# Probabilities times values by pairs of heads, 64 stationary columns each, in a fused attention and ELU feed-forward kernel

## The chip, the core and the metric

The kernel runs on one core of a Trainium2 chip. The core has five engines with queues of their own, each worked off in order: TensorE (PE, with its loads of stationary operands shown as PEld), VectorE (DVE), ScalarE (ACT), GpSimd (POOL) and SyncE (SP), which in this kernel issues all DMAs. The metric is the device time of one execution in microseconds, the median of several runs.

## The reference

Causal attention with a decay bias that is summed along the sequence, then a feed-forward layer with ELU on its result:

```python
B, H, S, D = q.shape                     # 8, 8, 576, 64
scores = q @ k.T / sqrt(D)
cum = cumsum(maximum(s, 0), -1)          # s: one number per head and position
bias = -(cum[..., :, None] - cum[..., None, :])
scores = where(causal, -1e9, scores + minimum(bias, 0))
attn = exp(scores - max(scores)); attn /= sum(attn) + 1e-9
x = (attn @ v) laid out as (4608 tokens, 512)
h = x @ w_in                             # 512 -> 2048
g = where(h > 0, h, exp(minimum(h, 0)) - 1)
out = g @ w_out                          # 2048 -> 512
```

All inputs and the output are float32.

## The kernel before

**How the order is made.** Every piece of work is written as an operation with a priority, one or more ways to do it (an engine, a planned cost in ns, and the code), the buffers it reads and those it writes (`op`). `Plan.issue` then runs a list scheduler on the host while the program is built: it picks, again and again, the operation that could start first by its planned times, takes the cheapest way, and writes the instructions down in this order. The chip sees only the result: a fixed order on each engine. A DMA is planned with a cost on SP (`SP_COST`, 430 ns, or 1250 ns for a transposing one) and a landing time (`LAG`, 1800 ns, plus bytes over `RATE`); a later operation that needs the data is placed after that. If the chip lands the data later than planned, the engine that reads it stands, and so does all that stands behind it in that engine's queue.

**Attention.** The first 320 positions of the first three batches (`Low`) are done in float32. All else goes by units (`Unit`): for each batch and pair of heads one unit for the first 64 positions of both heads (`h` is None), then one for each head with its blocks of 128 query rows: four blocks in batches 3 to 7 ("full", 20 pairs), the last two in batches 0 to 2 ("late", 12 pairs). A unit is prepared (loads of k and q, split into high and low parts), scored (`scoring`: matmuls into a PSUM bank, mask and minimum on DVE at L967, exponential on ACT at L972, then in `halved` the probabilities as two float16 halves, high on POOL, DVE or ACT, low mostly on DVE at L1025, interleaved into a tile `p16`, and turned by a transposing DMA into a tile `T`, L383), and weighed (`weighing`): the product with the values. There are two `T` buffers (`N_T`).

**The product.** `pair_values` splits the values of a pair of heads into float16 high and low parts, `v[:, head, key block, part, 64]`. In `weighing`, `keys(kb)` takes both parts of one head, 128 columns, as the stationary operand, and moves the high and then the low half of the probabilities past it. So PSUM rows 0 to 63 of `av` collect what the high values give and rows 64 to 127 what the low values give, and each head has 9 matmuls (L1084): two for each of four blocks of 128 keys, and one for the last 64 keys, whose halves lie in one tile. `halves` then adds the two halves of `av` into the half of the result tile `x` that belongs to the head: one instruction that scales and moves the other half (ACT at L1143 or DVE at L1145), one on DVE that scales and adds its own (L1148). After the second head `x` goes to DRAM.

**Scales.** `group_values` loads the values of a whole batch (a group) into a buffer of their own, `va`, kept in the place of a weight tile that is no longer needed: four such places (`w_all`) in turn. `scales_of` finds the group's largest value for a power of two: a maximum for each partition on DVE (`own`, L593), out to DRAM (`aside`), back into all partitions (`every`), and there the maximum and its exponent on DVE (L596, L598, L582).

**Feed-forward.** Tokens go in 12 chunks of 384. The weights are split into float16 parts, and each product is three matmuls: `hidden` (L1304, 384 columns), the ELU on ACT (L1268, L1275), `h` and `gg` on DVE and ACT (L1313, L1317, L1322), `project` (L1341, 512 columns), and the copy-out (L1372, L1373). The first chunk is done in float32 (L1288, L1333). These matmuls have the lowest priority: they fill PE where attention isn't ready.

## Time and profile before

| | |
|---|---|
| median of 3 runs | 1136.91 us (1136.84 to 1140.44) |
| profiled execution | 1139.71 us, its span 1137.9 us |
| mean granted TensorE clock | 0.981 |
| busy time of PE, DVE, ACT, POOL | 1052.2, 897.2, 651.3, 509.0 us |
| AV matmuls (L1084, tile `T`) | 576, 20 x 2 x 9 in full units, 12 x 2 x 9 in late ones |
| feed-forward matmuls in float16 | 2112 of 384 columns, 1584 of 512 |

The full units run from about 135 to 807 us, the late ones to 1023 us, and what is left of the feed-forward to the end. A row of a table of groups gives the line, the engine, the operation, what is written and read with its shape, the count, then busy time in us and mean ns of one; a matmul's mean is longer than its pace, because matmuls overlap. A row of waits names who waited for whom, with the total in us, how often, and the longest. An engine's name with a q behind it (SPq) is its sequencer.

### The profile page before, as it was taken

The page shows a single profiled execution, that of the slowest core. Times are in us where ns is not written, and L with a number is a line of the kernel's source. Part 1 is how long each engine was busy: PE and PEld are TensorE (multiplying, and loading weights), DVE is VectorE, ACT ScalarE, POOL GpSimd, SP SyncE. Part 2 cuts the span into 40 slices and gives each one's busy share as a digit, 9 for nine tenths or more (in the row PEclk, how much of TensorE's full clock was granted, in tenths as well). Part 3 has the DMA queues.
Part 4 walks back from the last instruction along what each step waited for, and adds up shares of the span by engine and source line. Part 5 has one row for each costly group of instructions (what it writes and reads, how often), then busy time and mean ns, then how long its engine had stood idle before and what let it go on. Part 6 is the DMA issues. An engine that isn't in the chain of part 4 may idle for free. (4 is left out here: it accounts for less than half of the span.)

```text
span 1137.9 us, 19124 instructions
## 1 busy us (share of the span) xinstructions
PE 1052.2 (92%) x5650; PEld 618.8 (54%) x5650; DVE 897.2 (79%) x2250; ACT 651.3 (57%) x1513; POOL 509.0 (45%) x756
## 2 busy tenths in 40 slices
PE   8799998798799989999899879999999999999998
PEld 7676554354455545545455535555556555555554
DVE  7788987898877878988698778888899898962433
ACT  4686765555454656556466555666665565554443
POOL 5542345925445454645455435555564553520000
PEclk9899999999999999999999989999999999999999
DMA  7687886473675685665666556566657666540000
GB/s 168 184 233 214 210 225 149 126 195 96 150 144 87 171 168 137 135 165 126 125 160 157 115 150 147 132 142 150 140 137 164 129 156 148 115 110 10 29 1 28
DMA packets 307160, 157.22 MB, mean 138 GB/s; under 512 B 226648, under 2 KB 281840, under 8 KB 307056
## 3 DMA queue, kind: packets, MB, share of 16 engines
q1 hardware_dynamic: 307056, 156.00, 58.3%
q8 instruction: 45, 0.74, 0.3%
q14 instruction: 59, 0.48, 0.2%
HBM read 80.38 MB, written 19.32 MB: 88 GB/s over the span
## 5 line engine op out<-in xcount | busy, mean ns | idle before, releaser
L1304 PE MATMUL h<-xh,wp 128*128 128x384 f16 x1408 | 394.1, 328 | 25.1 <-DVE gg L1322 24.9
L1341 PE MATMUL o<-wp,gg 128*128 128x512 f16 x1584 | 394.9, 386 | 2.3 <-DVE gg L1319 1.8
L1304 PEld LDWEIGHTS <-wp 128*128 128x128 f16 x2112 | 195.9, 98 | 176.5 <-issue 41.0
L1341 PEld LDWEIGHTS <-gg 128*128 128x128 f16 x1584 | 148.1, 99 | 160.7 <-issue 11.7
L1304 PE MATMUL h<-xl,wp 128*128 128x384 f16 x704 | 230.5, 327 | 3.8 <-POOL xl L1254 3.7
L972 ACT ACTIVATE p<-p,mn 128x192 f32<-128x192 f32 (+1 forms) x232 | 144.3, 622 | 89.7 <-DVE mn L967 86.1
L1268 ACT ACTIVATE g<-h,cs 128x384 f32<-128x384 f32 x176 | 101.9, 579 | 142.1 <-PE h L1304 140.0
L1313 DVE SCALAR_TENSOR_TENSOR h<-g,cs,h 128x384 f32<-128x384 f32 x176 | 108.5, 617 | 77.9 <-ACT g L1275 76.6
L1025 DVE SCALAR_TENSOR_TENSOR p<-p,sm,p 128x512 f16<-128x512 f32 (+3 forms) x224 | 164.6, 754 | 4.1 <-POOL p L1017 2.5
L1317 ACT ACTIVATE gg<-h 128x384 f16<-128x384 f32 x160 | 78.2, 488 | 102.5 <-DVE h L1313 101.1
L1017 POOL TENSOR_SCALAR p<-p,sm 128x64 f16<-128x64 f32 (+3 forms) x130 | 88.0, 683 | 94.9 <-DVE sm L978 57.4
L964 PE MATMUL sc<-kh,qs 128*128 128x192 f32 (+2 forms) x272 | 117.0, 433 | 10.6 <-DVE mn L967 6.5
L967 DVE CUSTOM_DVE_ANT_0 p<-sc,maskw 128x192 f32<-128x192 f32 (+1 forms) x232 | 108.9, 480 | 16.2 <-PE sc L964 13.7
L1322 DVE SCALAR_TENSOR_TENSOR gg<-h,gg 128x384 f16<-128x384 f32 x176 | 97.0, 551 | 19.3 <-ACT gg L1317 17.2
L964 PE MATMUL sc<-k,q 128*128 128x192 f32 (+2 forms) x272 | 84.1, 314 | 11.8 <-DMA q<-qs 11.8
L1084 PE MATMUL av<-T,v 128*128 128x256 f16 (+5 forms) x576 | 84.0, 292 | 2.2 <-DMA T<-p 2.2
L1084 PEld LDWEIGHTS <-v 128*128 128x128 f16 x576 | 55.7, 99 | 40.1 <-issue 7.8
L1275 ACT ACTIVATE g<-g 128x384 f32<-128x384 f32 x143 | 74.7, 522 | 4.1
L411 POOL TENSOR_TENSOR k<-stk,kh 64x576 fp32r<-64x576 f32 x46 | 69.8, 1517 | 10.4 <-ACT kh L392 8.2
L964 PEld LDWEIGHTS sc<-kh,qs 128*128 128x128 f32 x272 | 52.1, 192 | 40.9 <-DVE mn L967 15.8
L390 POOL TENSOR_SCALAR qs<-stq 128x512 fp32r<-128x512 f32 (+1 forms) x39 | 23.3, 597 | 90.0 <-PE sc L964 45.3
L402 POOL TENSOR_SCALAR v<-va,scales 128x320 f16<-128x320 f32 x43 | 24.8, 583 | 84.7 <-PE av L1084 76.6
(174 smaller groups left out, 1571.8 us busy)
## 6 DMA issues: line engine op xcount, KB each, us to landing
stk<-in_kT_dram SPq DMA_DIRECT2D x64, 288.0 KB
va<-in_vb_dram SPq DMA_DIRECT2D x32, 320.0 KB
stq<-in_qT_dram SPq DMA_DIRECT2D x40, 256.0 KB
w_i<-in_w_in_dram SPq DMA_DIRECT2D x16, 512.0 KB
w_o<-in_w_out_dram SPq DMA_DIRECT2D x16, 512.0 KB
out_dram<-ost SPq DMA_DIRECT2D x32, 256.0 KB
x_dram<-x_None SPq DMA_DIRECT2D x20, 288.0 KB
q<-qs SPq DMA_DIRECT2D x40, 128.0 KB
```

The costliest lines, as they stand in the source:

```text
L964: pe_.matmul(view(sc.v[:, :cw]), l, r, start=n == 0, stop=n == len(pairs) - 1)
L967: op(prio, [("DVE", 84 + dve_p(cw), lambda i=i, sc=sc: dve.tensor_tensor_reduce(pt.v[:, i * cw : (i + 1) * cw], sc.v[:, :cw], mv(i * cw, c ...
L972: op(prio, [("ACT", 480 + w / 1.2, lambda: act.activation(pt.v[:, :w], pt.v[:, :w], AF.Exp, bias=mn.v[:, n - 1 : n], scale=-1.0, accum_out ...
L1017: ("Pool", 160 + 1.04 * n, lambda part=part: pool.tensor_scalar(part(t16, 0), own(part), sm.v[:, r], 1.0, ALU.mult, ALU.mult)),
L1025: ("DVE-SB", dve_2(n), lambda part=part: dve.scalar_tensor_tensor(part(t16, 1), own(part), sm.v[:, r], part(t16, 0), ALU.mult, ALU.subtract)),
L1084: op(prio, [("PE", cost, lambda m=m, operands=operands: pe_.matmul(av.v[:, dst], *operands(), start=first and m == 0, stop=last and m == l ...
L1268: op(side, [("ACT", act_c(TC) + (0 if native else 90), lambda: act.activation(g.v[:, :TC], hp.v[:, :TC], AF.Exp, scale=1.0 if native else ...
L1304: pe_.matmul(hp.v[:, :TC], weight_part(f, 0, part)[1]()[:, c * P : (c + 1) * P], xx.v[:, c, :TC], start=(c == 0 and m == 0), stop=(c == NC ...
L1313: op(side, [("DVE", dve_p(TC), lambda: dve.scalar_tensor_tensor(hp.v[:, :TC], g.v[:, :TC], by(2 if sign[0] else 1), hp.v[:, :TC], ALU.mult ...
L1317: ("ACT", act_c(TC), lambda: act.activation(gg.v[:, 0, :TC], hp.v[:, :TC], AF.Copy, scale=2.0**-DOWN)),
L1322: op(side, [("DVE", dve_p(TC), lambda: dve.scalar_tensor_tensor(gg.v[:, 1, :TC], hp.v[:, :TC], 2.0**-DOWN, gg.v[:, 0, :TC], ALU.mult, ALU. ...
L1341: pe_.matmul(acc[i].v, gg.v[:, g, tb], weight_part(f, 1, part)[1](), start=(f == 0 and m == 0), stop=(f == NF - 1 and m == 2),)
```

## The change

Five things are changed, in one edit.

1. The product of probabilities and values is made once for a pair of heads. The stationary operand is now one part of one head's values, 64 columns; head 0 writes PSUM rows 0 to 63 and head 1 rows 64 to 127 of one bank, so that each half lies on the 64 columns of the array that belong to these rows. The matmuls of the two heads alternate. For each block of 128 keys there are three products a head (high values with high probabilities, high with low, low with high; low with low is left out), for the last 64 keys two. All 28 matmuls are one operation of the planner.
2. `av` then holds the finished result of both heads, in the rows where `x` wants them: one scaled copy of 128 rows (ACT or DVE, L1136 to L1140) in place of two instructions for each head. `halves` stays for the first 64 positions, without a scale.
3. `T` may also lie in the places of the third and fourth weight tile, once these were in use as weights; the values of groups then use only the first two (`% 2` in `group_values`).
4. The two DMAs of `scales_of` are planned with landing times of 5000 and 4500 ns instead of 1800, so is the write of the decay sums (5000).
5. Some planned costs and the planner's rule for VectorE's and GpSimd's shared use of a port (`PORT_LEAD`, 300 before, now 240 and 120) have other numbers.

```diff
-    PORT, PORT_LEAD = ("DVE-SB", "Pool"), 300.0
+    PORT_LEAD = {"DVE-SB": 240.0, "Pool": 120.0}
...
-        load(15, lambda: aux_dram.v[:, 0], sp, [(aux, 0)], [(aux_dram, 0)], NB * S * 4)
+        load(15, lambda: aux_dram.v[:, 0], sp, [(aux, 0)], [(aux_dram, 0)], NB * S * 4, lag=5000.0)
...
-        op(prio, [("DVE-SB", 30.0 + 70 * n, largest)], used, [own])
-        load(prio, lambda: aside.v.rearrange("n p -> p n"), lambda: own.v, [own], [aside], P * n * 4)
+        op(prio, [("DVE-SB", 60.0 + 70 * n, largest)], used, [own])
+        load(prio, lambda: aside.v.rearrange("n p -> p n"), lambda: own.v, [own], [aside], P * n * 4, lag=5000.0)
         load(prio, lambda: every.v, lambda: aside.v.rearrange("n p -> (n p)").partition_broadcast(P),
-             [aside], [every], P * P * n * 4)
-        op(prio, [("DVE-SB", 300.0 + 130 * n, exponents)], [every], [own, (scales, dst)])
+             [aside], [every], P * P * n * 4, lag=4500.0)
+        op(prio, [("DVE-SB", 500.0 + 130 * n, exponents)], [every], [own, (scales, dst)])
...
-        home = w_parts[NG - 1] if at == 0 else w_all[(at - 1) % NG]
+        home = w_parts[NG - 1] if at == 0 else w_all[(at - 1) % 2]
...
-        u.pt = plan.buf(sb, [P, 1 + (u.turns[u.last] - 1) * u.n_blocks, P], F16, f"T_{u.tag}", tag="T", bufs=N_T)
+        u.pt = plan.buf(sb, [P, 1 + (u.turns[u.last] - 1) * u.n_blocks, P], F16, f"T_{u.tag}", tag="T", bufs=N_T,
+                        others=[(w_all[g].key[1], 1, lambda n: n > 0) for g in range(2, NG)], always=True)
...
-            def own():
-                return u.values.v[:, u.h, kb].rearrange("p a d -> p (a d)")
-            used = [(u.pt, i) for i in range(i0, last)] + [(u.values, (m, u.h)) for m in range(2)]
-            pairs = [(used, lambda m=m: (own(), part(m))) for m in range(1 + (kb < last))]
-            products(pe16(c), pairs, dst, kb == 0, kb == last)
-            if kb == last:
-                halves(prio, u.back, u.h, wq, u.x_part((u.h, first)), HB + P * first, av, 0)
...
+        if u.h == 0:
+            return []
+        pair = (u.first_head, u)
...
+                for kb in range(last + 1):
+                    dst = slice(wq - columns(kb), wq)
+                    for m, v in ((0, 0), (1, 0), (0, 1)) if kb < last else ((0, 0), (0, 1)):
+                        for w in pair:
+                            pe_.matmul(
+                                av.v[w.h * HB : (w.h + 1) * HB, dst], w.values.v[:, w.h, kb, v], part(w, kb, m),
+                                start=kb == 0 and m == 0 and v == 0, stop=kb == last and v == 1,
+                            )
+            cost = sum((3 if kb < last else 2) * (pe16(columns(kb)) + 4) for kb in range(last + 1))
+            op(prio, [("PE", 200 + cost, step)],
+               [(w.pt, i) for w in pair for i in u.blocks] + [(u.values, (m, h)) for m in range(2) for h in range(2)],
+               [av])
...
+                ("ACT", act_c(wq) + 90, lambda: act.activation(
+                    x.v[:, cols], av.v[:, :wq], AF.Copy, scale=scales.v[:, back])),
+                ("DVE", dve_p(wq), lambda: dve.tensor_scalar(
+                    x.v[:, cols], av.v[:, :wq], scales.v[:, back], None, ALU.mult)),
```

Three places show the new order. The names: `av_5_1_0` is the product of batch 5, pair 1, head 0; `T_5_1_0` its turned probabilities; `h_3_13` and `wp_3` belong to the feed-forward; the last number of a name only tells tiles apart. On PE, where the product of batch 5, pair 1 begins, before:

```order
L1304 LDWEIGHTS wp_3_2378
L1304 MATMUL h_3_13_5233<-xh_2276,wp_3_2378 128x384
L1084 LDWEIGHTS v_5_1_0_0_4731
L1084 MATMUL av_5_1_0_0_5248<-T_5_1_0_0_5117,v_5_1_0_0_4731 128x512
L1084 LDWEIGHTS v_5_1_0_0_4731
L1084 MATMUL av_5_1_0_0_5248<-T_5_1_0_0_5117,v_5_1_0_0_4731 128x512
L1084 LDWEIGHTS v_5_1_0_0_4731
L1084 MATMUL av_5_1_0_0_5248<-T_5_1_0_0_5117,v_5_1_0_0_4731 128x448
```

and after:

```order
L1312 LDWEIGHTS wp_2_2275
L1312 MATMUL h_3_11_5245<-xh_2252,wp_2_2275 128x384
L1126 LDWEIGHTS v_5_1_0_0_4532
L1126 MATMUL av_5_1_1_0_5264<-T_5_1_0_0_5003,v_5_1_0_0_4532 64x512
L1126 LDWEIGHTS v_5_1_0_0_4532
L1126 MATMUL av_5_1_1_0_5264<-T_5_1_1_0_5146,v_5_1_0_0_4532 64x512
L1126 LDWEIGHTS v_5_1_0_0_4532
L1126 MATMUL av_5_1_1_0_5264<-T_5_1_0_0_5003,v_5_1_0_0_4532 64x512
L1126 LDWEIGHTS v_5_1_0_0_4532
L1126 MATMUL av_5_1_1_0_5264<-T_5_1_1_0_5146,v_5_1_0_0_4532 64x512
```

The two heads' T now alternate row by row, into 64 rows each of one bank; before, head 1's nine came some 120 rows later, after other work, with a bank of their own. (In the changed kernel the feed-forward's lines stand 8 lower: L1312 is what L1304 was.)

On SP, around the scales of the last group (`own_18`), before:

```order
L378 DMA stq_7_0_None_0_7302<-in_qT_dram 128x128
L378 DMA aside_18_7314<-own_18_7306 128x1
L378 DMA stv_7_0_None_0_7329<-in_vb_dram 128x64
L378 DMA every_18_7348<-aside_18_7314 128x128
L378 DMA k2_0_192<-aux_dram_219 1x576 x2
L378 DMA q2s_184<-qs_7_0_None_0_7379 64x128
```

and after:

```order
L378 DMA aside_18_9709<-own_18_9703 128x1
L378 DMA q2_0_190<-qs_1_0_0_2_9711 64x256
L378 DMA stk_1_0_1_2_9728<-in_kT_dram 128x576
L378 DMA stq_1_0_1_2_9735<-in_qT_dram 128x2x128
L383 DMA_TRANSPOSE T_0_3_0_2_9788<-p16_0_3_0_2_2_9774 128x8x128
L378 DMA every_18_9802<-aside_18_9709 128x128
```

Four DMAs now stand between the way out and the way back, where one stood; and with two buffers for groups in place of four the trip is made in batch 0's late units, not in batch 6. On DVE, 17 rows stood between L593 and L596 of this group and now 28 do.

On DVE, where the result of batch 5, pair 1 is copied out, before:

```order
L1313 SCALAR_TENSOR_TENSOR h_3_15_5375<-g_3_15_5413,cs_3_3336,h_3_15_5375 128x384
L1145 TENSOR_SCALAR x_5_1_None_0_5143<-av_5_1_1_0_5416,scales_71 64x512
L1148 SCALAR_TENSOR_TENSOR x_5_1_None_0_5143<-av_5_1_1_0_5416,scales_71,x_5_1_None_0_5143 64x512
L1322 SCALAR_TENSOR_TENSOR gg_3_15_5440<-h_3_15_5375,gg_3_15_5440 128x384
L977 TENSOR_SCALAR sm_5_2_0_0_5356<-sm_5_2_0_0_5356 128x4
```

and after:

```order
L978 RECIPROCAL sm_5_2_0_0_5194<-sm_5_2_0_0_5194 128x4
L1019 TENSOR_SCALAR p16_5_2_0_0_0_5301<-p0_82,sm_5_2_0_0_5194 128x2x128
L1140 TENSOR_SCALAR x_5_1_None_0_4957<-av_5_1_1_0_5264,scales_71 128x512
L1025 SCALAR_TENSOR_TENSOR p16_5_2_0_0_0_5301<-p0_82,sm_5_2_0_0_5194,p16_5_2_0_0_0_5301 128x2x128
L1025 SCALAR_TENSOR_TENSOR p16_5_2_0_0_1_5303<-p1_84,sm_5_2_0_0_5194,p16_5_2_0_0_1_5303 128x3x128
```

The two instructions for head 1 (and two more for head 0, earlier) became one. Of these 32 copies the planner puts 20 on ACT and 12 on DVE, and it moves some work from POOL to DVE: over the program POOL has 112 instructions fewer, DVE 32 fewer and ACT 11 more.

More of the change, by code (lines that the diff above doesn't have):

```diff
@@ L208, in issue @@
                     if b.others and (b.always or not busy):
-                        for key, bufs, *most in b.others:
-                            if most and taken[key] > most[0]:
+                        for key, bufs, *rule in b.others:
+                            if rule and not rule[0](taken[key]):
                                 continue
@@ L237, in issue @@
             end = start + cost
-            if engine in self.PORT:
+            if engine in self.PORT_LEAD:
                 port = end
@@ L1130, in weighing, with part, heads, step @@
-        return [lambda kb=kb: keys(kb) for kb in range(last + 1)]
-    def halves(prio, back, h, n, dst, c0, av, a0):
+            return P * (last - i0) - HB * half
+        def part(w, kb, m):
+            c = columns(kb)
+            if kb == last:
+                return w.pt.v[:, 0, P - c :]
+            end = (1 + (2 * kb + m + 1) * w.n_blocks) * P
+            return w.pt.v.rearrange("p u q -> p (u q)")[:, end - c : end]
+        def heads():
+            def step():
+                for kb in range(last + 1):
[10 more added lines that the diff above has]
+               [av])
+            x, label = u.x_part(("rows", first))
+            back, cols = slice(u.back, u.back + 1), slice(HB + P * first, HB + P * first + wq)
+            op(prio, [
+                ("ACT", act_c(wq) + 90, lambda: act.activation(
+                    x.v[:, cols], av.v[:, :wq], AF.Copy, scale=scales.v[:, back])),
+                ("DVE", dve_p(wq), lambda: dve.tensor_scalar(
+                    x.v[:, cols], av.v[:, :wq], scales.v[:, back], None, ALU.mult)),
+            ], [av, (scales, u.back)], [(x, label)])
+            load(prio, lambda: x_dram.v[u.b, u.j][:, u.cols], lambda: x.v[:, u.cols], [x],
+                 [(x_dram, u.piece)], P * (u.cols.stop - u.cols.start) * 4)
@@ L1134, in halves @@
+        return [heads]
+    def halves(prio, h, n, dst, c0, av, a0):
         x = dst[0]
@@ L1136, in halves @@
         cols, here = slice(c0, c0 + n), slice(a0, a0 + n)
[L1137 to L1150 removed]
+        psum_copy(prio, n, lambda: x.v[own, cols], lambda: av.v[other, here], [av], [dst])
+        op(prio, [("DVE", dve_p(n), lambda: dve.tensor_tensor(
+            x.v[own, cols], av.v[own, here], x.v[own, cols], ALU.add))], [av], [dst])
     def attention():
```

37 lines of the change are left out of this document (9 added, 28 removed).

## The prediction, made before the changed kernel ran

> **What bounds the kernel now.** I read the busy shares first, then a table of two stretches, the waits, the timeline around the longest waits, and the chain of work for rates. The shares of the span and two of the rows in 40 slices:
>
> ```profile
> span 1137.9 us, 19124 instructions
> PE 1052.2 (92%) x5650; PEld 618.8 (54%) x5650; DVE 897.2 (79%) x2250; ACT 651.3 (57%) x1513; POOL 509.0 (45%) x756
> PE   8799998798799989999899879999999999999998
> DVE  7788987898877878988698778888899898962433
> ```
>
> PE is the bound: 1052 us busy of 1138. So there are two ways to gain: less PE work, or less of its 86 us of idle time. The stretch with full and late units, and the rest after the last of them (columns: width, then busy time and count of PE, PEld, DVE, ACT, POOL; the clock; the DMA share; GB/s):
>
> ```profile
> 165.00:1024.00 859.00, 795.05 (x4346) 454.39 (x4345) 725.88 (x1792) 493.75 (x1108) 434.77 (x594) 0.98 0.62 142
> 1024.00:1138.00 114.00, 109.85 (x591) 57.54 (x588) 38.27 (x65) 47.56 (x89) 2.15 (x3) 1.00 0.05 17
> ```
>
> 64 us of the idle time lie in the first, where DVE is busy for 84% too; the second is almost pure PE. What is waited for (total us, times, longest):
>
> ```profile
> PE h L1304 <- DVE gg L1322: 24.9, 12, 7.0
> PE sc L964 <- DMA q<-qs: 11.8, 3, 4.2
> PE sc L964 <- DVE mn L967: 6.5, 9, 1.6
> PE sc L964 <- DVE pc_None L1035: 3.3, 1, 3.3
> PE av L1084 <- DMA T<-p: 2.2, 3, 0.8
> DVE own L596 <- DMA every<-aside: 18.0, 5, 6.4
> SPq L378 <- DMA aside<-own: 33.1, 7, 6.8
> ```
>
> PE waits mostly for DVE, and DVE itself stands for 18 us behind the exponents of a group's scales. The timeline shows how that reaches PE (start, duration; in brackets the idle time before and who ended it), once at 644 and once at 275 us:
>
> ```profile
> 643.90 0.37 SPq L378 DMA_DIRECT2D aside<-own  x1
> 644.32 0.43 SPq L378 DMA_DIRECT2D stv_None<-in_vb_dram  x1
> 650.92 0.33 SPq L378 DMA_DIRECT2D every<-aside  x1
> ...
> 649.90 0.18 DVE L978 RECIPROCAL sm<-sm 128x4 f32<-128x4 f32 x1
> 656.51 0.29 DVE L596 TENSOR_REDUCE own<-every 128x1 f32<-128x128 f32 x1 [6.43 <-DMA every<-aside]
> ...
> 659.92 0.48 PE L1304 MATMUL h<-xh,wp 128*128 128x384 f16 x1 [6.97 <-DVE gg L1322]
> ...
> 274.69 0.44 SPq L378 DMA_DIRECT2D aside<-own  x1
> 282.49 0.33 SPq L378 DMA_DIRECT2D every<-aside  x1
> 287.60 0.29 DVE L596 TENSOR_REDUCE own<-every 128x1 f32<-128x128 f32 x1 [2.91 <-DMA every<-aside]
> 289.82 0.74 PE L964 MATMUL sc<-kh,qs 128*128 128x448 f32 x1 [3.35 <-DVE pc_None L1035]
> ```
>
> The way out to DRAM takes 7.0 and 7.8 us from issue until SP may issue the way back, which takes another 5.6 and 5.1 us. The planner allows 2 x (0.43 + 1.8) = 4.5 us for the 12.6 to 12.9 us. Since queues run in order, SP stands from 644.75 to 650.92 with every later load behind it, DVE stands 6.43 us with h and gg behind it, and PE loses 6.97 us.
>
> **The AV products.** The chain of work gives their pace, the other rows the tail of a short matmul and the loads of stationary columns (busy us, mean ns):
>
> ```profile
> 733.16 1.28 PE av L1084 x9
> 860.12 0.85 PE av L1084 x9
> ...
> L1084 PE MATMUL av<-T,v 128*128 128x64 f16 x64 | 12.3, 193 | 0.0
> ...
> L1084 PEld LDWEIGHTS <-v 128*128 128x128 f16 x576 | 55.7, 99 | 40.1 <-issue 7.8 <-DMA T<-p 1.7 <-DMA k2s<-aux_dram 1.1
> L1288 PEld LDWEIGHTS h<-x,wa 128*128 128x128 f32 x128 | 23.7, 194 | 13.3 <-issue 4.4
> ...
> 9.19 5.43 PEld L1404 LDWEIGHTS scratch<-ident 128*128 128x128 f32 x48
> ```
>
> A head of four blocks moves 2 x (512 + 448 + 320 + 192) + 64 = 3008 columns in 1.28 us, one of two blocks 2 x (3 x 256 + 192) + 64 = 1984 in 0.85 us: 0.43 ns a column, weight loads hidden. A pair costs 2.56 us (20 pairs) or 1.70 us (12 pairs), 71.6 us in all. After, a pair of heads needs 28 half-width matmuls instead of 18 full ones, because high and low values are no longer in one stationary tile (low times low is dropped): 6 x 1472 + 4 x 64 = 9088 columns, or 6 x 960 + 4 x 64 = 6016.
>
> No row of this trace has a stationary tile of 64 columns, so I bound it. If the two halves of the array work side by side, half the columns count: 1.95 and 1.29 us, that is -0.61 x 20 - 0.41 x 12 = -17.1 us. If they don't, 3.91 and 2.59 us: +1.35 x 20 + 0.89 x 12 = +37.7 us. I take side by side, since the two heads of each round write disjoint output rows from disjoint columns of the array and nothing in the rows makes one wait for the other, but with two costs of its own. First, two weight loads a round: the f32 row has 48 loads of 128 columns in 5.43 us, 0.11 us each, so 64 columns are at most 0.055 and a round at least 0.11 us. That leaves the wide rounds alone (0.22, 0.19, 0.14 us) and stretches those of 192 and 64 columns: 3 x (0.22 + 0.19 + 0.14) + 3 x 0.11 + 2 x 0.11 = 2.20 us, and for two blocks 9 x 0.11 + 3 x 0.11 + 2 x 0.11 = 1.54 us; -0.36 x 20 - 0.16 x 12 = -9.1 us. If half-width f16 loads are as quick as the f16 row (99 ns in all against 194), they hide and -17.1 stands; I take the f32 price because the loads then decide and the careful end costs only 8 us. Second, entering and leaving half-width work may empty the array: a 64-column matmul lasts 193 ns and streams for 28, so a break costs up to 0.165 us; one for each of 32 blocks is 5.3 us. The term is -9.1 + 5.3 = -3.8 us, between -17.1 and +37.7.
>
> The Trainium skill bears on both costs. Its page "TensorEngine Tiling (Array Packing)", section "Restrictions", says that column tiling disables Fast Weight Load, which speaks against this change: by it the f32 price holds and the term is -3.8; were it wrong, about -11.8. The f16 and f32 rows above agree that there are two speeds; no run so far shows which one a half tile gets. The same page, section "Key Properties", says that a change of tiling mode drains the array, which is the break; no row here shows one. The page "TensorE: Matmul & The Clock Gate", Part 3, gives a span of one matmul plus about 4 ns for each further tile; by that alone the term is -17.1 and the sum near 1108 us, which stands among the rivals.
>
> **Copying the result out.** What two instructions for each head did becomes one for a pair:
>
> ```profile
> L1148 DVE SCALAR_TENSOR_TENSOR x_None<-av,scales,x_None 64x512 f32<-64x512 f32 x40 | 29.9, 747 | 4.3 <-ACT x_None L1143 3.5
> L1148 DVE SCALAR_TENSOR_TENSOR x<-av,scales,x 64x256 f32<-64x256 f32 x24 | 11.6, 481 | 1.4 <-ACT x L1143 0.9
> L1145 DVE TENSOR_SCALAR x_None<-av,scales 64x512 f32<-64x512 f32 x14 | 10.5, 747 | 8.5 <-PE av L1084 8.3
> L1145 DVE TENSOR_SCALAR x<-av,scales 64x256 f32<-64x256 f32 x7 | 3.3, 477 | 1.3 <-PE av L1084 1.2
> L1143 ACT ACTIVATE x_None<-av,scales 64x512 f32<-64x512 f32 x26 | 17.8, 684 | 11.6 <-PE av L1084 11.3
> L1143 ACT ACTIVATE x<-av,scales 64x256 f32<-64x256 f32 x17 | 8.0, 470 | 9.8 <-PE av L1084 9.6
> ...
> L1025 DVE SCALAR_TENSOR_TENSOR p<-p,sm,p 128x64 f16<-128x64 f32 x30 | 12.0, 400 | 0.8 <-POOL p L1017 0.7
> L854 DVE SCALAR_TENSOR_TENSOR v<-va,scales,v 128x320 f16<-128x320 f32 x36 | 25.2, 712 | 0.3
> ```
>
> DVE gives up 55.3 us and ACT 25.8. The new order has 12 copies on DVE and 20 on ACT: 8 x 0.747 + 4 x 0.477 = 7.9 and 12 x 0.684 + 8 x 0.470 = 12.0 us, with the free size the same and 128 rows in place of 64. DVE is then handed work that POOL had (15 more of 64 columns, 10 more of L854, and about 25 others, at L854's price): 6 + 7 + 18 = 31 us. Net DVE loses about 55.3 - 7.9 - 31 = 16 us. None of it lies on PE; its worth is what PE waits for DVE: 24.9 + 6.5 + 3.3 = 34.7 us, less the 10.3 of the two stalls above, 24 us. DVE's slack in the long stretch grows from 133 to 149 us, and with waits inverse to slack that is -11%: -3 us (bounds 0 and -24).
>
> **Longer landing times.** Two trips through DRAM are now planned with 0.43 + 5.0 + 0.43 + 4.5 = 10.4 us instead of 4.5. In the new order DVE has 28 rows instead of 17 between the last group's maximum and its exponents, and SP four instead of one between out and back. The two stalls cost PE 6.97 + 3.35 = 10.3 us, and 10.4 covers most, not all, of 12.6; I take 0.8 of it, -8 us (bounds 0 and -18, all of DVE's wait at this place). The three waits for q, 11.8 us, stay: that load keeps its landing time. Values prefetched into two buffers instead of four still leave a group's length, some 100 us at the pace of PE's order, for a trip of 13; I cost that at nothing. So too the planner's other new numbers: they change a row's planned cost by 30 to 300 ns, and no stand above hangs on one of these rows.
>
> **Holding a pair.** Both heads' T must now live until the pair's products. For the first three pairs there are two T buffers in all, so the next head's turned loads wait for the products; behind them on SP stand q and k loads. PE waited 2.2 us for T so far; FFN products fill in. I take +1 us, bounds 0 and three stands of SP like the one of 6.2 us above, +18.5.
>
> **Sum.** -3.8 - 3 - 8 + 1 = -13.8 us. The profiled execution took 1139.7 (span 1137.9 and 1.8 around it), so 1125.9; it was itself 2.8 us over the median of 1136.9, from which the same steps give 1123. About 0.3% is what this kernel's measurement can tell from no change.
>
> **Rivals.** (a) The halves take turns: in this trace every matmul starts only as its predecessor's columns end (9 in 1.28 us), and both heads contract over the same 128 rows of the array. Then AV is +37.7 instead of -3.8: 1164 us, slower. It decides as soon as less than half of the columns overlap. (b) Partly side by side: every round waits for its loads in the open, some 0.06 us over 14 rounds: 27 us against -17, near +10, and the other gains cancel it: 1137, the same. (c) Loads hide and nothing breaks: AV -17.1, sum -27: 1110. (d) The landing times are still too short: the trip out lasted up to 7.8 us against 5.0; SP still stands, and 8 becomes 3 us: 1128, inside the forecast.
>
> **Numbers.** Forecast (halves overlap, loads or breaks cost some; 1112 to 1133) 0.62; (c) and better, under 1112, 0.12; (b), 1133 to 1141, 0.10; (a) and anything above, 0.16. Faster by over 0.3% (below 1133.5): 0.73; within: 0.10; slower: 0.17. The range 1104 to 1146 leaves out most of (a) and the end of (c), about 0.2.
>
> **What would show it.** Right: 28 AV matmuls in 1.95 to 2.4 us with starts of the two heads close together; PE busy 4 to 15 us lower; the wait of own for every under 5 us, and SP's for aside under 20; DVE near 880 us busy. Wrong: AV bursts of over 2.6 us, starts of equal spacing; new rows of PE waiting for T, or for DVE as much as before.

## The result and the profile after

The changed kernel takes 1126.24 us (median of 6 runs, 1122.94 to 1130.43); the kernel before, run beside it, 1137.47 us: a ratio of 0.9906, interval 0.9881 to 0.993. Measured once more in a later batch (e9, below) it was 0.9921, 0.9892 to 0.995. The forecast was 1123.

The total came out as forecast, its parts did not, so part of the hit is luck (more of that below). The page of the changed kernel, the same four rows as before (the profiled execution took 1122.94 us, the shortest of its runs):

```profile
span 1121.1 us, 19607 instructions
PE 1036.3 (92%) x5970; PEld 614.3 (55%) x5970; DVE 856.2 (76%) x2218; ACT 646.5 (58%) x1525; POOL 422.4 (38%) x644
PE   8799998557999899988999989899989999999998
DVE  7698895986888797897897798688879898643433
```

PE is 15.9 us less busy (1052.2 before), DVE 41. PE's idle time, span less busy, was 85.7 us and is 84.8: it did not fall. In the row of slices PE has two fives side by side near 220 us that were not there before. What is waited for (total us, times, longest):

```profile
PE sc L964 <- DVE mn L967: 33.5, 12, 16.7
PE h L1312 <- DVE gg L1330: 15.4, 13, 4.9
PE av L1126 <- DMA T<-p: 6.6, 2, 5.1
PE sc L964 <- DMA q<-qs: 2.0, 2, 1.1
POOL p L1017 <- DMA T<-p: 29.2, 8, 7.3
SPq L378 <- DMA aside<-own: 25.8, 6, 6.8
SPq L383 <- DMA aside<-own: 1.7, 1, 1.7
```

The row in which DVE's own waits for every (18.0 us before) is gone: the longer landing times did what they say. In its place PE stands 33.5 us for DVE's mn, 16.7 of it at one stop, and waits for T (6.6, before 2.2). SP still stands 27.5 us for aside (33.1). The timeline of the long stop (start, duration, in brackets the idle time before and who ended it):

```profile
216.01 2.28 PE L1349 MATMUL o<-wp,gg 128*128 128x512 f16 x9 [0.47 <-ACT gg L1325]
216.47 12.66 DVE L650 SCALAR_TENSOR_TENSOR wp<-wa,scales,wp 128x512 f16<-128x512 f32 x19
229.06 2.99 DVE L574 TENSOR_REDUCE peaks<-va 128x1 f32<-128x640 f32 x4
234.99 0.50 PE L964 MATMUL sc<-kh,qs 128*128 128x192 f32 x1 [16.70 <-DVE mn L967]
237.65 0.48 POOL L1017 TENSOR_SCALAR p<-p,sm 128x256 f16<-128x256 f32 x1 [25.43 <-issue]
```

In the new order DVE makes 19 low parts of weights and four peaks in one go, 15.6 us, while the block minimum that PE's scores wait for stands behind them. This is the plan, not chance: the same stop of 16.7 us is in every profile of this order (e4, e5, e8, e9).

The AV blocks by the chain of work, and the groups behind them:

```profile
689.34 2.05 PE av L1126 x28
778.40 1.41 PE av L1126 x28
```

```profile
L1126 PE MATMUL av<-T,v 128*64 128x256 f16 (+5 forms) x896 | 63.0, 291 | 6.6 <-DMA T<-p 6.6
L1126 PEld LDWEIGHTS <-v 128*64 128x64 f16 x896 | 46.5, 111 | 31.7 <-issue 19.6 <-DMA stq_None<-in_qT_dram 0.3 <-DMA stq<-in_qT_dram 0.3
L1138 ACT ACTIVATE x_None<-av,scales 128x512 f32<-128x512 f32 x12 | 8.2, 681 | 4.3 <-PE av L1126 4.3
L1140 DVE TENSOR_SCALAR x_None<-av,scales 128x512 f32<-128x512 f32 x8 | 6.0, 749 | 15.2 <-PE av L1126 15.2
L1138 ACT ACTIVATE x<-av,scales 128x256 f32<-128x256 f32 x8 | 3.7, 463 | 0.6 <-PE av L1126 0.6
L1140 DVE TENSOR_SCALAR x<-av,scales 128x256 f32<-128x256 f32 x4 | 1.9, 481 | 0.4 <-PE av L1126 0.4
```

A full pair takes 2.05 us in place of 2.56, a late one 1.41 in place of 1.70. Single records show how (a round is one matmul of head 0 and the one of head 1 behind it): in the block at 340.64 us the first matmuls of head 0 and head 1 start at 340.643 and 340.646, the next two at 340.883 and 340.886, and at the narrow end rounds of 192 columns start every 82 ns. Both heads' matmuls run at once, 3 to 4 ns apart, and so do their two weight loads.

### The profile page after: what moved, and what is told of

Read it like the earlier page. It is cut to its first block, busy times and chain, and to the rows that moved or that the text cites. A ratio compares the mean times of both kernels' runs of the same rounds, so it can differ in the third digit from the quotient of the medians.

```text
span 1121.1 us, 19607 instructions
## 1 busy us (share of the span) xinstructions
PE 1036.3 (92%) x5970; PEld 614.3 (55%) x5970; DVE 856.2 (76%) x2218; ACT 646.5 (58%) x1525; POOL 422.4 (38%) x644
## 5 line engine op out<-in xcount | busy, mean ns | idle before, releaser
L1312 PE MATMUL h<-xh,wp 128*128 128x384 f16 x1408 | 394.7, 331 | 16.1 <-DVE gg L1330 15.4
L1349 PE MATMUL o<-wp,gg 128*128 128x512 f16 x1584 | 389.7, 383 | 4.1 <-ACT gg L1325 3.4
L1312 PEld LDWEIGHTS <-wp 128*128 128x128 f16 x2112 | 200.1, 99 | 171.0 <-issue 34.0
L1349 PEld LDWEIGHTS <-gg 128*128 128x128 f16 x1584 | 146.6, 99 | 161.8 <-issue 7.1
L1312 PE MATMUL h<-xl,wp 128*128 128x384 f16 x704 | 232.5, 330 | 0.9 <-DVE xl L1265 0.9
L1025 DVE SCALAR_TENSOR_TENSOR p<-p,sm,p 128x512 f16<-128x512 f32 (+3 forms) x247 | 174.9, 728 | 10.1 <-ACT p L1021 7.5
L964 PE MATMUL sc<-kh,qs 128*128 128x192 f32 (+2 forms) x272 | 118.5, 438 | 34.4 <-DVE mn L967 33.5
L1017 POOL TENSOR_SCALAR p<-p,sm 128x512 f16<-128x512 f32 (+3 forms) x120 | 84.8, 712 | 159.1 <-DVE sm L978 50.4
L411 POOL TENSOR_TENSOR k<-stk,kh 64x576 fp32r<-64x576 f32 x37 | 56.7, 1533 | 39.5 <-ACT kh L392 32.1
L1126 PE MATMUL av<-T,v 128*64 128x256 f16 (+5 forms) x896 | 63.0, 291 | 6.6 <-DMA T<-p 6.6
L1021 ACT ACTIVATE p<-p,sm 128x512 f16<-128x512 f32 (+3 forms) x98 | 55.9, 585 | 17.1 <-DVE sm L978 4.5
L1126 PEld LDWEIGHTS <-v 128*64 128x64 f16 x896 | 46.5, 111 | 31.7 <-issue 19.6
L411 POOL TENSOR_TENSOR qs<-stq,qs 64x512 fp32r<-64x512 f32 (+1 forms) x44 | 52.6, 1196 | 19.7 <-ACT qs L392 16.0
```

Source lines behind the costliest of these rows:

```text
L411: ("Pool", pool_2(n), lambda: pool.tensor_tensor(dst(), src(), hi(), ALU.subtract)),
L964: pe_.matmul(view(sc.v[:, :cw]), l, r, start=n == 0, stop=n == len(pairs) - 1)
L1017: ("Pool", 160 + 1.04 * n, lambda part=part: pool.tensor_scalar(part(t16, 0), own(part), sm.v[:, r], 1.0, ALU.mult, ALU.mult)),
L1025: ("DVE-SB", dve_2(n), lambda part=part: dve.scalar_tensor_tensor(part(t16, 1), own(part), sm.v[:, r], part(t16, 0), ALU.mult, ALU.subtract)),
L1126: pe_.matmul(av.v[w.h * HB : (w.h + 1) * HB, dst], w.values.v[:, w.h, kb, v], part(w, kb, m), start=kb == 0 and m == 0 and v == 0, stop=kb ...
L1312: pe_.matmul(hp.v[:, :TC], weight_part(f, 0, part)[1]()[:, c * P : (c + 1) * P], xx.v[:, c, :TC], start=(c == 0 and m == 0), stop=(c == NC ...
```

## The experiments

Each ratio is to runs of the kernel before on the same chip in the same batch. Where two kernels of one batch are compared, the ratio of their ratios is given, with the widest ends that the two intervals allow. For the profiles I split the span in three: PE's work at full clock, what half clock added, and idle time. The second is worked out from the records of the granted clock: after stops of PE it falls to 0.5 for 3.4 us or a multiple, and half of PE's busy time in these stretches counts as lost, which is an estimate. Each row is one execution. The changed kernel stands there twice, and its two rows differ by 2.1, 4.0 and 2.8 us; the runs of one kernel lie 3 to 15 us apart.

| profile | span | PE's work | lost to half clock | idle |
|---|---|---|---|---|
| before | 1137.9 | 1032.5 | 19.7 | 85.7 |
| changed kernel | 1121.1 | 1016.7 | 19.6 | 84.8 |
| e9, changed kernel again | 1116.4 | 1018.8 | 15.6 | 82.0 |
| e1, pairs alone | 1134.7 | 1019.6 | 25.1 | 90.0 |
| e2, planner's numbers alone | 1138.0 | 1027.9 | 25.1 | 85.0 |
| e8, changed, full-width AV | 1127.9 | 1026.3 | 19.1 | 82.5 |
| e10, before, scales over PE | 1127.7 | 1036.5 | 12.2 | 79.0 |
| e12, pairs alone, scales over PE | 1090.7 | 1021.2 | 10.7 | 58.8 |
| e11, changed, scales over PE | 1086.6 | 1017.2 | 10.8 | 58.6 |

**e1: the pairs alone.** The changed kernel with the planner's old numbers, so that the pairs, their single copy-out and the places for T (points 1 to 3 of the change) are left:

```
-    PORT_LEAD = {"DVE-SB": 240.0, "Pool": 120.0}
+    PORT_LEAD = {"DVE-SB": 300.0, "Pool": 300.0}
-        load(prio, ... aside ..., lag=5000.0)
+        load(prio, ... aside ...)
```

(and so for every and the other edited costs.)

> The changed kernel with the planner's old numbers: landing times of 1800 ns, old costs, PORT_LEAD 300 for both. So only the pairs of heads, the single copy-out and the places for T are left of the change. Theory: the AV blocks pace is a matter of the array, so 28 matmuls take 2.05 and 1.41 us as in the changed kernel, which with 0.1 us on entering each is -10 us of PE against before; the order has no long run of L650 on DVE, so the 16.7 us stop of PE near 218 us is not there; DVE's waits for the way back through DRAM stay (some 10 to 20 us). Time 1120 to 1126 us. Rival (the pairs bring nothing, the landing times all): 1135 to 1140.

1135.26 us, 1.0013 (0.9993 to 1.0032): no gain. PE's work fell by 12.9 us, but idle time rose by 4.3 and half clock took 5.4 more, each hardly more than two executions of one kernel can differ. Waits:

```profile
DVE own L596 <- DMA every<-aside: 18.2, 4, 6.4
PE sc L964 <- DMA aside<-own: 4.0, 1, 4.0
PE av L1126 <- DMA T<-p: 4.3, 2, 3.0
```

**e2: the planner's numbers alone**, on the kernel before: the same lines the other way.

> The kernel before with the planner's new numbers alone: landing times of 5000 and 4500 ns, the new costs, PORT_LEAD 240 and 120; AV as before, head by head. Theory: DVE no longer waits for the way back (18 us before, under 5 now), which is worth about 8 us of PE, and its order has no long run of L650: 1126 to 1132 us. Rival (longer landing times only move the waiting elsewhere): 1135 to 1140; second rival (the new PORT_LEAD itself brings the 17 us stop): a stop of over 10 us near 210 us and 1140 or more.

1135.19 us, 1.002 (0.9998 to 1.0042): no gain either. DVE's wait of 18.0 us is gone here too, and something else is late:

```profile
PE sc L964 <- DMA q<-qs: 15.3, 4, 6.7
```

Neither half is worth anything by itself and both together save 10 to 11 us, so the parts do not add.

**e3: the old lead on the shared port**, in the changed kernel (only the first two lines of e1's edit).

> The changed kernel with one number undone: PORT_LEAD 300 for both engines again. Theory: the 16.7 us stop of PE near 218 us is 19 low weight parts (L650) in a row on DVE with the softmax behind them; in this kernel's order no more than five stand in a row, the stop goes, and nothing else of size changes: 1108 to 1114 us. Rival (the stop comes from holding T for a pair, or DVE's work has to be done there in any case): 1122 to 1128 us with a stop of the same size within 30 us of it.

1121.22 us, 0.9889 (0.9866 to 0.9913), within the first interval of the changed kernel and just under that of e9. Here the 19 weight parts are spread out and the stop of 16.7 us is gone, yet the span of its profile is 1122.2, since others came:

```profile
PE h L1312 <- DVE gg L1330: 23.9, 20, 5.8
PE sc L964 <- DVE mn L967: 12.7, 14, 3.4
PE av L1126 <- DMA T<-p: 7.5, 3, 4.1
```

So taking the long stop away in this manner brings nothing, and the 1108 to 1114 us that were expected did not come.

From e1 to e3 only the landing times and a few planned costs change, with the same lead, on the same chip in the same batch: 1135.26 to 1121.22 us, a ratio of 0.988 (0.983 to 0.992). So the numbers that bring nothing on the kernel before (e2) are worth 14 us on the pairs.

**e4: the halves in turn.** All 14 matmuls of head 0, then all 14 of head 1; everything else in the same order:

```
-                for kb in range(last + 1):
...
-                        for w in pair:
+                for w in pair:
+                    for kb in range(last + 1):
```

> The changed kernel with the loops of the AV block turned: all 14 matmuls of head 0, then all 14 of head 1, same count, same tiles, same order of everything else. Theory (halves overlap only where matmuls that follow each other lie in different halves): blocks of 3.8 to 3.9 us and 2.5 to 2.6 us instead of 2.05 and 1.41, that is +1.8 x 20 + 1.1 x 12 = +49 us of PE, 1160 to 1180 us. Rival (half-width matmuls are cheap by themselves, whatever the neighbour): blocks and time unchanged within 1%.

1160.05 us in one run; what counts here are the blocks. The blocks by the chain of work:

```profile
712.05 3.78 PE av L1126 x27
804.32 2.50 PE av L1126 x27
```

This is the price of rival (a), 3.91 and 2.59 us, nearly met: 3.78 against 2.05 us from nothing but the order of the rows. The two halves overlap only where neighbours in the order go to different halves.

**e8: full width in the same order.** The block as 18 matmuls of 128 columns. This kernel leaves out the separation of the heads (both heads' products are added into one bank), so its result is not the product and only its times are used:

```
-                    for m, v in ((0, 0), (1, 0), (0, 1)) if kb < last else ((0, 0), (0, 1)):
+                    for m in range(1 + (kb < last)):
                         for w in pair:
                             pe_.matmul(
-                                av.v[w.h * HB : (w.h + 1) * HB, dst], w.values.v[:, w.h, kb, v], part(w, kb, m),
+                                av.v[:, dst], w.values.v[:, w.h, kb].rearrange("p a d -> p (a d)"), part(w, kb, m),
```

> The changed kernel's order, but a pair's AV block is 18 matmuls of 128 stationary columns for each pair of key blocks' worth of work (both value parts and both heads in one bank, 128 rows wide, one behind the other) instead of 28 of 64 columns that run two at a time; part of the computation is changed: the two heads' products are added into one bank. Copy-out and everything else are the same. By the measured blocks (before 2.55 us a full block from first start to next instruction and 28 ns behind it, after 2.05 plus 0.19 at its two ends) each of 20 full blocks takes 0.3 to 0.4 us longer and each late one 0.15 to 0.2, PE is 8 to 11 us busier, and as 27 of the 32 pairs' blocks have other work behind them the time is 5 to 10 us longer: 1131 to 1136 us. Rival (the block's pace is not on the path, the plan around it is): PE busier by 8 to 11, time within 3 us of 1126. Breaks: with 128 columns the step into and out of a block is near 28 ns instead of 126 and 256.

1131.9 us, 0.9988 (0.9968 to 1.0009), that is 0.7 to 0.8%, or 8 to 9 us, above the changed kernel's two ratios, as the first theory has it; against the second measurement the ends are 0.2 and 1.2%. This compares batches: the changed kernel was not run beside e8, and e5 (below), which was and which has half-width blocks, came out as high. So the gain rests on the records of the blocks and less on this difference. The blocks:

```profile
694.18 2.56 PE av L1126 x18
781.64 1.70 PE av L1126 x18
```

From the start records, with the same neighbours in both: first matmul to next instruction 2.551 against 2.052 us, late 1.698 against 1.414; the step from the instruction ahead 163 against 256 ns (216 against 309 behind L1349); the step out 29 against 126 to 128, which is inside the block's time. So a block of half width pays 93 ns at its start and 97 at its end, 0.19 us, and still saves 0.406 us net (0.191 late): 20 x 0.406 + 12 x 0.191 = 10.4 us. What is left of the change beside that, in this kernel, is 0.9988: nothing that can be told from zero. But that is one way to divide it up. Going from e1 to the changed kernel, the pairs come first and bring nothing (1.0013), and the numbers bring all of it.

**Where the rest went: aside.** The way out to DRAM is 128 writes of 4 bytes for each of eight sets of scales, and 384 for a ninth. By the semaphore records it lands 8 to 10 us after its issue in the changed kernel, and transfers issued meanwhile land only with it or later (mean us from issue to landing, with their number; the last two columns are all others):

```
                      T behind aside   q behind aside    other T     other q
before                6.6 (10)         5.1 (3)           3.4 (198)   2.4 (61)
changed kernel        8.5 (14)         9.4 (2)           3.5 (194)   2.5 (62)
e3, old lead          7.6 (15)         6.6 (5)           3.4 (193)   2.5 (59)
e5, aside on ACT      8.6 (12)         9.9 (2)           3.4 (196)   2.5 (62)
```

The planner gives T and q 1.8 us and the time for their bytes. Planning aside itself with 5.0 puts other work, and with it more T, behind it.

**e5 and e6: aside from ACT's queue**, in the changed kernel and in e3's:

```
-        load(prio, ... aside ..., lag=5000.0)
+        op(prio, [("SP", SP_COST, lambda: nc.scalar.dma_start(...), 5000.0, P * n * 4)], [own], [aside])
```

> The changed kernel, with one edit: the small DRAM write of each group's peaks (aside) is issued from ACT's queue and no longer from SP's; order and planned times are the same. Theory (transfers of one queue that are issued behind aside wait until it has landed): the T that are issued within its 8 to 10 us land in about 3.5 us instead of a mean of 8.5 (14 of them), q in about 2.5 instead of 9.4; PE's wait for T (6.6 us) and q2s and q (4.7 us) goes, and what waits on late T elsewhere; 1117 to 1123 us, ratio to the kernel before near 0.986. [...] Rival 1 (it is the DMA engines that are busy with 128 packets of 4 bytes, not the queue): the landings behind aside stay at 7 to 10 us, and the time at 1126. Rival 2 (PE's 16.7 us stop at the row of low weight parts and the half clock behind it are the whole loss): landings fall, PE's wait for T goes, but the time stays within 3 us of 1126, since FFN work is only done earlier and is missing later.

> The same edit (aside from ACT's queue) on the kernel with the pairs and the new landing times but the old lead on the shared port of 300 ns for both engines, 1121.2 us in the last batch. Theory: PE's wait for T (7.5 us there) and q (3.1) goes, 1112 to 1118 us, ratio near 0.982. Rival 1 (DMA engines busy): landings behind aside unchanged, 1121. Rival 2 (a wait that goes here is only moved to the FFN matmuls that covered it): PE's wait for gg ahead of the hidden matmuls (23.9 us) grows by what T gives, 1119 to 1122.

My theory that the order of one queue does it is refuted. The transfers went through a queue of their own, as the page shows, and T behind them landed no sooner (table above; in e6 a mean of 7.0):

```profile
q10 hardware_dynamic: 1552, 0.01, 0.1%
PE av L1127 <- DMA T<-p: 8.2, 2, 5.0
PE sc L965 <- DMA kl<-aux_dram: 6.8, 1, 6.8
PE av_None L1086 <- DVE pc_None L418: 4.8, 1, 4.8
```

e5 took 1133.47 us, 0.9986 (0.9964 to 1.0007), slower than the changed kernel by its ratios. It has a stop of 6.8 us for kl, keys of the float32 part (2.5 at most in the changed kernel), and that is the same hold once more: ACT issues this aside at 20.9 us, ahead of a load of kl at 22.6, which lands just behind it, at 29.7; in the changed kernel SP issues it at 23.3, behind that load. The stop of 4.8 for pc_None, at 178 us, stands where the changed kernel has one of 4.2 for mn. What else makes e5 slow was not settled. e6 took 1123.5 us, 0.9904 (0.9866 to 0.9942), the same as e3. The Trainium skill's page "DMA: Bandwidth & Descriptors", section "Queues, rings and completion order", would have said so: both issuers' rings lie on the same 16 engines, and the increment of a semaphore lands only after every earlier write of its engine, across its queues. The rows agree. That the engines are simply busy with the small writes, the rival of e5, is out by the records of e6's transfers. Aside is issued at 619.66 us, its packets of 4 bytes are through by 621.2, and hardly anything moves from 622.5 on (the last two figures of a row of windows are the DMA engines' busy share and GB/s):

```profile
619.66 0.33 ACTq L603 DMA_DIRECT2D aside<-own  x1
620.30 0.35 SPq L378 DMA_DIRECT2D stq_None<-in_qT_dram  x1
626.00:627.00 1.00, 0.00 (x0) 0.00 (x0) 0.00 (x0) 0.00 (x0) 0.00 (x0) 1.00 0.00 0
627.00:628.00 1.00, 0.00 (x0) 0.00 (x0) 0.00 (x0) 0.00 (x0) 0.00 (x0) 1.00 0.00 0
```

Yet the 16 increments of aside's semaphore come one by one from 624.27 to 628.37 us, and those of the load behind it, on SP's queue, from 624.42 to 628.56, most of them 0.15 to 0.2 us after one of aside's (624.27 and 624.42, 625.34 and 625.52, 625.60 and 625.78). PE stands too. What holds the small writes so long the records do not show.

**e7, e10, e11, e12: the scales without DRAM.** PE turns the partial peaks, DVE takes maximum and exponent, and a matmul with ones spreads them over the partitions:

```
-        load(prio, ... aside from own ...)
-        load(prio, ... every from aside, to all partitions ...)
-        op(prio, [("DVE-SB", 500.0 + 130 * n, exponents)], [every], [own, (scales, dst)])
+        op(prio, [("PE", 120.0, lambda: pe_.transpose(tr.v[:n, :P], own.v, ident))], [own], [tr])
+        op(prio, [("DVE", 500.0, exponents)], [tr], [red])
+        op(prio, [("PE", 120.0, lambda: pe_.matmul(bc.v[:, :n], ones_row[:n], red.v[:n, 1:], ...))], [red], [bc])
+        op(prio, [("DVE", 350.0, spread)], [bc], [own, (scales, dst)])
```

e7 is e3 with it:

> Pairs, new landing times, old lead of 300 ns, and the groups' scales without any transfer: PE turns the 128 partial peaks (one transpose), DVE takes the maximum of the row and the power of two, and PE spreads it over the partitions by a matmul with ones, where before a write to DRAM and a broadcast read (18 transfers, 8 to 15 us each) did it. Theory (aside's transfer both holds SP's queue and makes the scales late): T and q never take over 7 us, the scales are ready some 15 us earlier in each of the 9 places, chunk starts don't wait; PE gets 18 small instructions of 0.1 to 0.3 us and the waits ahead of them; 1108 to 1117 us. Rival (the new plan's own waits: PE stands still at the transpose and at the ones matmul until DVE is through, 9 times two waits of 0.5 to 2 us, and DVE is in a row of weight parts): 1120 to 1130.

1101.2 us, 0.9717 (0.9691 to 0.9742). To learn whose gain that is, the same went into the kernel before (e10), the whole change (e11) and the pairs alone (e12), with the changed kernel as it is beside them (e9):

> The changed kernel itself once more, beside the three others, since the last batch gave 1133.5 to the same order with another queue for aside, where 1126.2 had been measured. Theory (a kernel with aside in it differs from run to run by what a landing of 7 to 12 us meets, and the first measurement stands on 6 runs): ratio 0.988 to 0.996 to the kernel before. Rival (the queue of ACT did cost): 0.9906 again within 0.002.

> The kernel before with one change: the scales of a group of rows go over PE (turn, maximum, ones matmul) and not through DRAM. AV blocks, landing times, costs and port lead as before. Theory (aside's transfer is what held the time up in every version, beside the AV pace): DVE's wait for every (18.0 us) goes, idle falls from 85.7 to 65 to 72, some 10 us of half clock go; 1108 to 1118 us, and so the pairs keep 8 to 14 us of the difference to the 1101.2 measured with pairs, landing times and PE scales. Rival (the pairs' banks and the landing times are what made the room): 1125 to 1135.

> The changed kernel whole (port lead 240 and 120 ns) with the scales over PE. Theory (without aside the plan is kept more nearly, and the 19 low weight parts in a row at 218 us were an accident of one plan): 1098 to 1106 us, within 4 us of the same with the old lead (1101.2). Rival (the new lead puts DVE's weight parts in a row in every plan): a PE stop of 10 us or more stays, 1106 to 1114.

> Pairs alone (old landing times, old costs, old port lead) with the scales over PE. With it the pairs have a price of their own where no aside is in the way: theory: 8 to 14 us below the kernel before with PE scales, since PE's AV blocks are some 10 us shorter and nothing else takes them back, and within 4 us of 1101.2 since the landing times had mostly aside's to set right; 1098 to 1106. Rival (each order has its own stops, and the pairs' 10 us are lost as they were with aside, 1135.3 against 1133.5): within 3 us of the kernel before with PE scales.

| | scales through DRAM | scales over PE |
|---|---|---|
| before | 1 | 0.9955 (0.9933 to 0.9976), 1127.16 us |
| pairs alone | 1.0013 (0.9993 to 1.0032) | 0.9664 (0.9634 to 0.9693), 1094.51 us |
| the whole change | 0.9921 (0.9892 to 0.995), 1123.19 us | 0.9613 (0.9588 to 0.9639), 1088.95 us |

The page's first rows of e10, e12 and e11, in this order:

```profile
span 1127.7 us, 19233 instructions
PE 1048.7 (93%) x5673; PEld 619.1 (55%) x5673; DVE 901.1 (80%) x2261; ACT 652.9 (58%) x1526; POOL 505.8 (45%) x755
```

```profile
span 1090.7 us, 19695 instructions
PE 1031.9 (95%) x5993; PEld 611.4 (56%) x5993; DVE 872.0 (80%) x2232; ACT 626.5 (57%) x1493; POOL 471.3 (43%) x710
```

```profile
span 1086.6 us, 19718 instructions
PE 1028.0 (95%) x5993; PEld 613.5 (56%) x5993; DVE 863.4 (79%) x2240; ACT 644.2 (59%) x1514; POOL 431.1 (40%) x662
```

Without the trip the pairs alone are worth 0.971 (0.966 to 0.976), 33 us, and the whole change 0.966 (0.961 to 0.970), 38 us, where with it they are worth nothing and 10 to 11. My expectation for e10, that the trip held up every version alike, is refuted: the kernel before gains only 5.6 us from its removal. The trip costs little while PE has other limits, and takes most of the gain once these are gone. The pairs alone are here, as in e1, the pairs with their copy-out and the places for T. By the table of spans they save, without the trip, 15.3 us of PE's work and 20.2 us of idle time; with it (e1) 12.9 and -4.3. What PE waits for shows who gave way (all rows of the waits added up by the engine waited for, us):

```
                          DVE     DMA    POOL   ACT
before                    48.1    16.6    8.5   6.4
changed kernel            56.9    14.7    3.6   3.9
e10, before               55.0     5.3    8.2   4.3
e12, pairs alone          42.5     0.7    5.7   1.3
e11, whole change         40.8     3.3    8.9   0.7
```

The new instructions themselves are cheap. PE's turn waits long only once, in e11 at 195 us, for DVE, which is again in a row of 12 low weight parts and four peaks:

```profile
PE tp L610 <- DVE mn L974: 13.3, 1, 13.3
```

```profile
L612 PE MATMUL bc<-red,ones_row 1*128 1x1 f32 (+1 forms) x18 | 3.6, 266 | 1.0 <-DVE red L602 0.8 <-DVE sm L984 0.3
L610 PE MATMUL tp<-ident,own 128*1 128x128 f32 (+1 forms) x9 | 2.6, 283 | 13.3 <-DVE mn L974 13.3
```

So the long stop of DVE outlives the trip, as the rival of e11 had it, and the time is better than both nevertheless: 1088.95 us is the best version of this study, 4% below the kernel before. How much of a difference is the lot of one plan, e7, e11 and e12 show: with pairs and scales over PE in all three, and only the planner's numbers between them, they lie 12 us apart (1088.95, 1094.51 and 1101.2; ratios 0.9613, 0.9664 and 0.9717). That is as much as the whole change was worth with the trip, and a third of the 33 to 38 us that it is worth without. e9 gave 1123.19 us and so the first theory's range; that the slowness of e5 is its own is likely, but the two were not run in one batch.

Not settled: why DVE's release of PE improves by 12.5 us with the pairs when the trip is gone (e10 to e12) and gets worse with it. DVE has 29 us less to do in e12 than in e10, much of it the copies, but no run changed the copies alone, nor the places for T.

## Why the prediction came out right, and what was wrong in it

**The AV products**: mechanism right, size off. Forecast -3.8 us, measured -10.4 in the blocks (e8 against the changed kernel). Halves work side by side (e4 is the counter-test). The step that failed is the first of the two costs, that two loads of a round follow one another and stretch rounds of 192 and 64 columns: the loads of the two halves start 3 to 4 ns apart, and rounds of 82 ns go on with loads of 110 ns in them, so loads of one half overlap its matmuls as well. A load of 64 columns is indeed no quicker than one of 128 (111 ns against 99 before). The Trainium skill's page "TensorEngine Tiling (Array Packing)" lets one expect that in "Restrictions", where column tiling turns off Fast Weight Load. It changed nothing in the time. The block itself comes out at 2.05 us less the 0.097 of its last step, 1.955, the 1.95 of "loads hide". The second cost, one break a block of up to 0.165 us, 5.3 in all, measured 0.19 and 6.1 us. The drain at a change of mode, of which the same page of the Trainium skill speaks in "Key Properties", fits that; no run takes the break apart. The rule of some 4 ns for each further tile, of the Trainium skill's page "TensorE: Matmul & The Clock Gate", Part 3, holds for the starts; taken alone, without the breaks, it gave -17.1 (and a sum of 1110, as in rival (c), not the 1108 that stands beside it).

**Copying out**: the counts and durations held (12 on DVE at 749 and 481 ns, 20 on ACT at 681 and 463). DVE lost 41 us where 16 were forecast: what the planner gave it for that added 6 us net and not 31 (L1025 10.3 more, 174.9 against 164.6; L854 2.9 more; other groups less), so the step that failed is to price the 25 unnamed instructions like L854: they stood at 18 us and came to about nothing. The 3 us that PE should have gained by it did not appear: with the trip in place PE waits longer for DVE, 56.9 us against 48.1.

**Longer landing times**: forecast -8 us. By themselves they are worth nothing that shows (e2 1.002), on the pairs 14 us (e1 to e3). The mechanism went half the way: DVE's wait of 18.0 us is gone, as forecast under 5. But SP's stand is 27.5 us, not under 20. The step that failed is to price the trip by what stands for it alone and to leave the loads around it as they were ("the three waits for q stay": they are 2.0 us in the changed kernel and 15.3 in e2). The trip did not only come late itself, it held back what was issued behind it, and a plan that knows of the trip's own time alone puts more there. This is rival (d) by another road: not the 12.6 us against 10.4, but T and q that take 8 to 9 us against the 1.8 planned.

**Holding a pair**: PE's wait for T rose by 4.4 us against +1, within the bounds; the two slots of the first three pairs had no visible part in it, since 5.1 of the 6.6 us is one wait at 718 us, for a T issued behind the aside of 713.7 us.

**The sum**: -13.8 was forecast and about -10 came. Divided up by e8 it is -10.4 by AV, where -3.8 stood, and about nothing by the rest, where -10 stood, and the two errors cancelled. Divided up by e1 the pairs bring nothing and the numbers all. So the step that failed is the sum itself: each term was priced on the kernel before, as if it kept its worth beside the others. With 12 us between plans that differ in a few numbers alone, a total within 3 us of the forecast is luck; what was understood is that the halves run side by side and that DVE's wait for the way back goes. Rivals (a) and (b) are out, (c) had the loads right and the breaks wrong. Three of the marks under "what would show it" held (starts close together, blocks of 2.05 us, own's wait gone), three missed (PE 15.9 us less busy instead of 4 to 15; DVE 856 instead of 880; SP 27.5 instead of under 20), and two signs of being wrong came as well: PE waits more for T, and for DVE as much as before (56.9 us against 48.1).

## What to carry to other kernels

Two stationary tiles of 64 columns pay when their matmuls alternate in the order, two by two with equal sizes, and in blocks long enough for two breaks of some 0.1 us; the same rows in turn took 84% longer (e4's 3.78 us against 2.05). Before a plan is tuned for a late transfer, look at what lands behind it: here a tiny write to DRAM with 4 bytes a row delayed the loads issued behind it, and another queue for it did not help, while doing the small exchange on PE did. When a change to the limiting engine brings nothing by itself, try it again with the next limit out of the way: here the pairs, with their copy-out and the places for T, were worth nothing with the trip and 33 us without. And do not add up terms that were each priced alone.

## What was not expected of the hardware

Matmuls and weight loads of the two column halves start 3 to 4 ns apart and run fully side by side down to rounds of 82 ns; entering and leaving such a block costs 93 and 97 ns. A write of 128 times 4 bytes to DRAM takes 8 to 10 us and holds back landings of transfers from another queue too (8.6 us against 3.4 in e5), even while the DMA engines stand idle (e6, from 626 to 628 us). After stops of PE the granted clock is 0.5 for 3.4 us or a multiple; this cost 19.7 us of the kernel before and 10.8 of e11, so that a stop costs more than its length.
